# Memory attention and a squared-ReLU MLP: padded state rows with whole-tile weight halves, and the squared ReLU kept in PSUM

## The chip, the cores and the metric

The kernel runs on one core of a Trainium2 chip. Its metric is device time in microseconds (us) of one execution. The engines of a core work side by side, each through its own queue in order: TensorE (PE, with its weight loads as PEld), VectorE (DVE), ScalarE (ACT), GpSimd (POOL) and SyncE (SP), which here only issues DMAs.

## The reference

```python
scale = 1.0 / np.sqrt(D)                     # x: (8, 8, 512, 64), state: (8, 8, 32, 64): B, H, S or N, D
a  = softmax(scale * x @ state.T)            # rows of x read the state
a2 = softmax(scale * state @ x.T)            # rows of the state read x
attn = concat([a @ state, a2 @ x], axis=2)   # (8, 8, 544, 64)
h = attn.transpose(0, 2, 1, 3).reshape(8 * 544, 512) @ w_in    # w_in (512, 2048)
g = np.maximum(h, 0.0) ** 2
out = g @ w_out                              # w_out (2048, 512)
```

Both softmaxes subtract the row's maximum and add 1e-9 to the sum. x, state and the output are float32; the weights arrive as float64.

## The kernel before

TensorE multiplies float32r, a shortened float32, at full speed. So a factor that must be exact is divided into hi, the value rounded to float32r, and lo, the rest; a product becomes hi·hi + lo·hi + hi·lo. The helper `split` does it: ACT casts into hi, another engine subtracts to get lo.

The rows of x never pass through `a @ state` followed by w_in. Instead z = state @ w_in is formed for each head, and up(x) = a @ z. `z_part(G, k, g)` makes one part of z: G is the group of four batches (0: batches 0 to 3, 1: batches 4 to 7), k one of 8 blocks of 256 columns of w_in, g one of two halves of the rows. For G = 0 its `convert` turns the float64 words of w_in into float32 (`singles`: one ACT and four VectorE instructions, lines 106 to 116) and keeps the result in DRAM (`wd`); for G = 1 it is loaded from there. `cut` divides the weights: a tile w2 of 128 rows holds, for one head of a pair, hi of that head's 64 rows and lo of the same rows in the other 64. `product(i)` multiplies it with the state: once with stz_lo and once with stz_hi, both of which hold the state twice, in rows 0 to 63 and again in 64 to 127 (`z_state`). So each product of the array adds hi and lo of the weights. The first six parts of G = 0 are `plain`: one float32 product, undivided. z goes to DRAM (`zd`) and comes back, re-ordered, by `z_fetch`.

The MLP works in units. A unit is 128 of the 2048 columns of h for one batch: `up` adds six products of 128x512 into the PSUM tile ph (pool ps_h, two buffers). Then ACT takes the ReLU into r in SBUF, the square follows in place (ACT in the first ten units, then VectorE at line 383), and `split` gives g_hi (ACT) and g_lo. g_lo is computed by VectorE, in the first, third and fifth unit by POOL. r, g_hi and g_lo have two buffers each. `down` adds twelve products of 128x512 into four tiles po, two units later: eight that read g_hi, four that read g_lo. Batches 0 and 1 are done in pieces, `BOTH`, while the weights are still being converted: 2 units of batch 0, 6 of batch 1, 14 of batch 0, 10 of batch 1. The last 16 units are half as wide and do the state's own rows.

`wo_load` converts w_out in the same way as w_in (tile wof). Steps that are not units (conversion, z, attention of the coming batches) are handed out between units by two lists with due times, `weights` and `reads`. This gives the program's order; a scheduler then fixes each engine's queue from it and from its own timing of instructions, so an edit in one place can move instructions in others. The tags and pools set which buffers a step waits for: w2_0 and w2_1 have two buffers, wf two.

Of the kernel before, what the change touches and what calls it, by code (L numbers as in the profile page):

```python
# [18 lines left out]
def memory_attention_then_relu2_ffn(  # L19
# [21 lines left out]
    nc = tc.nc  # L41
# [80 lines left out]
    def z_state(G):  # L122
        if G == 0:
            raw = const.tile([P, H, GB * N], F32, name="st_f")
            st["raw"] = raw
        else:
            raw = sb.tile([P, H, GB * N], F32, name="st_raw", tag="raw", bufs=RAW)
        src = stT.rearrange("d (h b n) -> d h b n", h=H, b=B)[:, :, G * GB:(G + 1) * GB, :]
        for j in range(2):
            nc.sync.dma_start(  # L130
                out=raw[j * D:(j + 1) * D].rearrange("d h (b n) -> d h b n", b=GB), in_=src
            )
        hi = sb.tile([P, H, GB * N], F32R, name="stz_hi", bufs=1)
        lo = sb.tile([P, H, GB * N], F32R, name="stz_lo", bufs=1)
        split(hi, lo, raw, nc.gpsimd)
        st[G] = hi, lo

    def z_part(G, k, g):

        box = {}  # L140
        ccs = slice(g * NCC // NG, (g + 1) * NCC // NG)
        nq = NCC // NG

        def load():
            if G:
                box["wf"] = sb.tile([P, nq, FW], F32, name="wf", bufs=2)
                nc.sync.dma_start(out=box["wf"], in_=wd[k][:, ccs, :])
                return
            raw = sb.tile([P, nq, FW, 2], I32, name="w_raw", tag="raw", bufs=RAW)
            nc.sync.dma_start(out=raw.rearrange("p c f w -> p (c f w)"), in_=w_in[k * NG + g])  # L150
            box["raw"] = raw

        def convert():
            wf = sb.tile([P, nq, FW], F32, name="wf", bufs=2)
            singles(wf, box["raw"])
            nc.sync.dma_start(out=wd[k][:, ccs, :], in_=wf)
            box["wf"] = wf

        plain = G == 0 and k * NG + g < PLAIN_Z

        def cut():
            if plain:
                return
            wf = box["wf"]
            w2 = []
            for i in range(2):
                own = slice(i * D, (i + 1) * D)
                other = slice((1 - i) * D, (2 - i) * D)
                w = sb.tile([P, nq, FW], F32R, name=f"w2_{i}", bufs=2)
                nc.scalar.copy(out=w[own], in_=wf[own])  # L170
                nc.gpsimd.tensor_sub(out=w[other], in0=wf[own], in1=w[own].bitcast(F32))  # L171
                w2.append(w)
            box["w2"] = w2

        def product(i):
            def run():
                own = slice(i * D, (i + 1) * D)
                pz = ps_x.tile([P, nq, FW], F32, name="pz", tag="px")
                for q in range(nq):
                    h = g * HG + 2 * q + i  # L180
                    if plain:
                        nc.tensor.matmul(
                            pz[:, q, :], lhsT=st["raw"][own, h, :], rhs=box["wf"][own, q, :],
                            start=True, stop=True,
                        )
                        continue
                    st_hi, st_lo = st[G]
                    w = box["w2"][i][:, q, :]
                    nc.tensor.matmul(pz[:, q, :], lhsT=st_lo[:, h, :], rhs=w, start=True, stop=False)  # L189
                    nc.tensor.matmul(pz[:, q, :], lhsT=st_hi[:, h, :], rhs=w, start=False, stop=True)  # L190
                if G == 0 and k == 0:
                    if g == 0 and i == 0:
                        z_first.append(sb.tile([P, NG, FW], F32, name="z_raw", bufs=2))
                    for q in range(nq):
                        at = (2 * q + i) * N
                        dst = z_first[0][at:at + N, g, :]
                        nc.scalar.copy(out=dst, in_=pz[:N, q, :])
                stage = sb.tile([P, nq, FW], F32, name="z_stage", bufs=4)
                nc.scalar.copy(out=stage, in_=pz)
                dst = zd[G, k].rearrange("p g (q i) f -> p g q i f", i=2)[:, g, :, i, :]  # L200
                nc.scalar.dma_start(out=dst, in_=stage)
            return run

        return load, convert, cut, [product(i) for i in range(2)]
# [161 lines left out]
    def mlp(width, fcs, first, rows, aux, at_end=None):  # L366

        nt = width // P
        po = []
        gs = {}  # L370
        last = len(fcs) - 1

        def up(fc):
            ph = ps_h.tile([P, S], F32, name="ph", tag="ph")[:, :width]
            todo = first(fc)
            for i, (w, v) in enumerate(todo):
                nc.tensor.matmul(ph, lhsT=w, rhs=v, start=i == 0, stop=i == len(todo) - 1)  # L377
            r = sb.tile([P, S], F32, name="r", bufs=2)[:, :width]
            nc.scalar.activation(r, ph, AF.Relu)  # L379
            if units[0] < 10:  # L380
                nc.scalar.activation(r, r, AF.Square)
            else:
                nc.vector.tensor_mul(out=r, in0=r, in1=r)  # L383
            units[0] += 1
            hi = sb.tile([P, S], F32R, name="g_hi", bufs=2)[:, :width]
            lo = sb.tile([P, S], F32R, name="g_lo", bufs=2)[:, :width]
            split(hi, lo, r, pool_early(units[0] < 6 and units[0] % 2))
            gs[fc] = hi, lo

        def down(i):  # L390
            fc = fcs[i]
            hi, lo = gs.pop(fc)
            if not po:
                po.extend(
                    ps_o.tile([P, DM], F32, name=f"po{t}", tag="po") for t in range(nt)
                )
            todo = [(t, j) for t in range(nt) for j in range(3)]
            if i < last:
                todo.sort(key=lambda tj: tj[1] == 2)
            for t, j in todo:  # L400
                g = (hi, hi, lo)[j][:, t * P:(t + 1) * P]
                w = wo[fc // FPC][j % 2][:, fc % FPC, :]
                nc.tensor.matmul(  # L403
                    po[t], lhsT=g, rhs=w, start=i == 0 and j == 0, stop=i == last and j == 2
                )

        for i in range(len(fcs) + 2):
            if i <= last:
                up(fcs[i])
                aux()  # L410
            elif i == last + 1 and at_end:
                at_end()
            if i >= 2:
                down(i - 2)
            if i <= last:
                aux()
        for t in range(nt):
            rows(t, po[t])
# [253 lines left out]
```

## Time and profile before

| What | Value |
|---|---|
| median of 3 runs | 738.25 us (737.76 to 740.44) |
| the profiled execution | 736.62 us; span from the first instruction to the last 734.8 us |
| mean granted TensorE clock | 0.97 |
| PE busy | 678.6 us (92%), 3112 instructions |
| DVE busy | 520.5 us (71%), 774 instructions |
| ACT busy | 403.1 us (55%), 720 instructions |
| POOL busy | 259.0 us (35%), 201 instructions |
| DMA moved | 94.71 MB, mean 129 GB/s |

Busy time is the union of an engine's instructions. In rows of instructions, "L97 DVE ... g_lo<-r,g_hi 128x512 ... x16 | 20.3, 1272 | 3.5" reads: line 97 on VectorE, output g_lo from inputs r and g_hi, 16 of them, 20.3 us in all, 1272 ns the mean of one, and 3.5 us in which the engine idled just before them. Line 97 is that of the helper `split`, so its rows are told apart by their tiles. Instructions of one engine that follow each other closely overlap a little at their ends, so their starts lie closer than their durations.

### The profile page before, as it was taken

To read this page: it belongs to the slowest core of one execution; us is meant where nothing else is said; L and a number is where in the kernel's file an instruction comes from. 1 tells how busy PE (TensorE), PEld (TensorE's weight loads), DVE (VectorE), ACT (ScalarE), POOL (GpSimd) and SP (SyncE) were. 2 spreads that over 40 slices of the span, in tenths; PEclk is the share of its full clock that TensorE was granted. 3 is DMA by queue.
4 is the path that set the end of the run, shared out by engine and by line. 5 is a ranking of instruction groups with operands and counts; after the bars stand their busy time and mean duration, and the time that the engine had idled before them with its cause. 6 is when DMAs were issued, how large, how long until landed. Compare 5 with 4: busy or idle time off the path is not lost.

```text
span 734.8 us, 9269 instructions
## 1 busy us (share of the span) xinstructions
PE 678.6 (92%) x3112; PEld 548.6 (75%) x3112; DVE 520.5 (71%) x774; ACT 403.1 (55%) x720; POOL 259.0 (35%) x201
## 2 busy tenths in 40 slices
PE   4877878868999999999999999999999999999994
PEld 2456666656788788888888888888888888888993
DVE  5998999895978789648854984498459745442542
ACT  3748696554666767677643653465345434332541
POOL 3456556664655763752250332033212400000000
PEclk9769999998999999999999999999999999999998
DMA  9878788555553653464232212221121102100420
GB/s 295 267 250 293 214 258 273 186 159 163 175 167 128 214 184 111 139 219 132 87 88 82 89 58 70 77 84 68 62 85 51 38 29 86 35 10 0 144 58 29
DMA packets 74163, 94.71 MB, mean 129 GB/s; under 512 B 3972, under 2 KB 55940, under 8 KB 74116
## 3 DMA queue, kind: packets, MB, share of 16 engines
q1 hardware_dynamic: 56708, 77.34, 33.1%
q10 hardware_dynamic: 17408, 16.78, 6.7%
q8 instruction: 24, 0.39, 0.2%
q14 instruction: 23, 0.19, 0.1%
HBM read 62.13 MB, written 31.98 MB: 128 GB/s over the span
## 4 chain that ended last, share of the span: by engine, by line
PE 67%; DVE 6%; DMA 3%; ACT 2%; issue 1%; POOL 0%; ACTq 0%; DVEq 0%; POOLq 0%; SPq 0%
PE po L403 41%; PE ph L377 21%; DMA z_raw<-zd 3%; PE pr L340 2%; PE pq L274 1%; DVE r L383 1%; DVE g_lo L97 1%; DVE wof L112 1%; PE pz L190 1%; PE pz L189 1%; DVE z_lo L97 1%; PE pt L328 1%; DVE wof L108 1%; DMA zd<-z_stage 0%; DVE wof L107 0%
## 5 line engine op out<-in xcount | busy, mean ns | idle before, releaser
L403 PE MATMUL po<-wo_hi,g_hi 128*128 128x512 f32 x544 | 215.1, 397 | 3.2 <-ACT wo_hi L96 2.2
L403 PE MATMUL po<-wo_lo,g_hi 128*128 128x512 f32 x544 | 214.7, 396 | 0.0
L383 DVE TENSOR_TENSOR r<-r 128x512 f32<-128x512 f32 (+1 forms) x134 | 112.4, 840 | 98.5 <-ACT r L379 98.4
L97 DVE TENSOR_TENSOR g_lo<-r,g_hi 128x512 fp32r<-128x512 f32 (+1 forms) x141 | 120.0, 852 | 64.4 <-PE po L403 44.9
L403 PE MATMUL po<-wo_hi,g_lo 128*128 128x512 f32 x544 | 156.6, 397 | 6.4 <-DVE g_lo L97 6.3
L379 ACT ACTIVATE r<-ph 128x512 f32<-128x512 f32 (+1 forms) x144 | 82.0, 572 | 119.0 <-PE ph L377 108.1
L96 ACT CAST g_hi<-r 128x512 fp32r<-128x512 f32 (+1 forms) x144 | 85.9, 597 | 90.3 <-DVE r L383 51.5
L403 PEld LDWEIGHTS po<-wo_hi,g_lo 128*128 128x128 f32 x544 | 101.0, 189 | 29.9 <-DVE g_lo L97 9.2
L403 PEld LDWEIGHTS po<-wo_hi,g_hi 128*128 128x128 f32 x544 | 102.9, 189 | 25.8 <-ACT wo_hi L96 2.8
L403 PEld LDWEIGHTS po<-wo_lo,g_hi 128*128 128x128 f32 x544 | 102.8, 189 | 21.7 <-issue 0.7
L171 POOL TENSOR_TENSOR w<-wf,w 64x512 fp32r<-64x512 f32 x52 | 79.1, 1521 | 45.0 <-ACT w L170 26.6
L377 PE MATMUL ph<-a_hi,z_hi 128*128 128x512 f32 x256 | 84.5, 408 | 8.1 <-ACT r L379 4.0
L377 PE MATMUL ph<-a_lo,z_hi 128*128 128x512 f32 x256 | 82.8, 399 | 0.0
L377 PE MATMUL ph<-a_hi,z_lo 128*128 128x512 f32 x256 | 82.1, 401 | 0.0
L97 POOL TENSOR_TENSOR xt_hl<-xt_raw,xt_hl 128x1024 fp32r<-128x1024 f32 x12 | 29.9, 2494 | 114.9 <-ACT xt_hl L96 87.4
L377 PEld LDWEIGHTS ph<-a_hi,z_hi 128*128 128x128 f32 x256 | 47.8, 193 | 19.8 <-ACT r L379 5.5
L97 POOL TENSOR_TENSOR xn_hl<-xn_raw,xn_hl 128x1024 fp32r<-128x1024 f32 x16 | 40.4, 2525 | 49.7 <-ACT xn_hl L96 49.0
L377 PEld LDWEIGHTS ph<-a_hi,z_lo 128*128 128x128 f32 x256 | 49.3, 194 | 10.7
L377 PEld LDWEIGHTS ph<-a_lo,z_hi 128*128 128x128 f32 x256 | 48.7, 192 | 10.8
L97 DVE TENSOR_TENSOR z_lo<-z_raw,z_hi 128x512 fp32r<-128x512 f32 x64 | 50.2, 785 | 7.6 <-ACT z_hi L96 7.6
L96 ACT CAST z_hi<-z_raw 128x512 fp32r<-128x512 f32 x64 | 39.4, 615 | 12.7 <-DMA z_raw<-zd 12.7
L97 POOL TENSOR_TENSOR a_lo<-at,a_hi 128x512 fp32r<-128x512 f32 x16 | 24.0, 1498 | 55.1 <-ACT a_hi L96 55.0
(125 smaller groups left out, 865.9 us busy)
## 6 DMA issues: line engine op xcount, KB each, us to landing
zd<-z_stage ACTq DMA_DIRECT2D x64, 256.0 KB
z_raw<-zd SPq DMA_DIRECT2D x63, 256.0 KB
xt_raw<-xT SPq DMA_DIRECT2D x16, 512.0 KB
w_raw<-w_in SPq DMA_DIRECT2D x16, 512.0 KB
wo_raw<-w_out SPq DMA_DIRECT2D x16, 512.0 KB
xn_raw<-xn SPq DMA_DIRECT2D x16, 512.0 KB
wd<-wf SPq DMA_DIRECT2D x16, 256.0 KB
wf<-wd SPq DMA_DIRECT2D x16, 256.0 KB
```

The costliest lines, as they stand in the source:

```text
L96: nc.scalar.copy(out=hi, in_=src)
L97: eng_lo.tensor_sub(out=lo, in0=src, in1=hi.bitcast(F32))
L108: nc.vector.tensor_scalar(out=bits, in0=bits, scalar1=3, scalar2=0x3FFFFFF8, op0=ALU.logical_shift_left, op1=ALU.bitwise_and,)
L112: nc.vector.scalar_tensor_tensor(out=bits, in0=high, scalar=-0x40000000, in1=bits, op0=ALU.bitwise_and, op1=ALU.bitwise_or,)
L171: nc.gpsimd.tensor_sub(out=w[other], in0=wf[own], in1=w[own].bitcast(F32))
L189: nc.tensor.matmul(pz[:, q, :], lhsT=st_lo[:, h, :], rhs=w, start=True, stop=False)
L190: nc.tensor.matmul(pz[:, q, :], lhsT=st_hi[:, h, :], rhs=w, start=False, stop=True)
L340: nc.tensor.matmul(pr[:, q].rearrange("p i c -> p (i c)"), lhsT=my["e"][:, t, q].rearrange("p i n -> p (i n)"), rhs=my["xn"][:, t, q].rear ...
L377: nc.tensor.matmul(ph, lhsT=w, rhs=v, start=i == 0, stop=i == len(todo) - 1)
L379: nc.scalar.activation(r, ph, AF.Relu)
L383: nc.vector.tensor_mul(out=r, in0=r, in1=r)
L403: nc.tensor.matmul(po[t], lhsT=g, rhs=w, start=i == 0 and j == 0, stop=i == last and j == 2)
```

## The change

For batches 0 to 3 (G = 0) the weights are divided once: w2_0 holds hi of all 128 rows, w2_1 holds lo, and `split` makes them with one ACT cast and one VectorE subtraction of 128x512. Before, ACT made two casts and POOL two subtractions of 64x512. The state is padded: stz_hi and stz_lo of a head hold the state in that head's own 64 rows and zeros in the other 64 (four memsets on POOL, and two casts and two subtractions on half the rows). Since a product no longer adds hi and lo of the weights by itself, there are three products a head: lo·hi, hi·hi, hi·lo. Batches 4 to 7 keep their way, and so do the six plain parts.

In the MLP the square is written back into the PSUM tile ph: ACT's Square reads r and writes ph in the first ten units, VectorE multiplies ph by r into ph in the others (a negative value times its ReLU is zero). `split` reads ph in place of r, always with VectorE.

```diff
--- before.py
+++ after.py
@@ -132,7 +132,15 @@
             )
         hi = sb.tile([P, H, GB * N], F32R, name="stz_hi", bufs=1)
         lo = sb.tile([P, H, GB * N], F32R, name="stz_lo", bufs=1)
-        split(hi, lo, raw, nc.gpsimd)
+        if G:
+            split(hi, lo, raw, nc.gpsimd)
+        else:
+            for i in range(2):
+                own = slice(i * D, (i + 1) * D)
+                other = slice((1 - i) * D, (2 - i) * D)
+                for v in (hi, lo):
+                    nc.gpsimd.memset(v[other, i::2, :].bitcast(F32), 0.0)
+                split(hi[own, i::2, :], lo[own, i::2, :], raw[own, i::2, :], nc.vector)
         st[G] = hi, lo
 
     def z_part(G, k, g):
@@ -162,15 +170,16 @@
             if plain:
                 return
             wf = box["wf"]
-            w2 = []
-            for i in range(2):
+            w2 = [sb.tile([P, nq, FW], F32R, name=f"w2_{i}", bufs=2) for i in range(2)]
+            box["w2"] = w2
+            if G == 0:
+                split(w2[0], w2[1], wf, nc.vector)
+                return
+            for i, w in enumerate(w2):
                 own = slice(i * D, (i + 1) * D)
                 other = slice((1 - i) * D, (2 - i) * D)
-                w = sb.tile([P, nq, FW], F32R, name=f"w2_{i}", bufs=2)
                 nc.scalar.copy(out=w[own], in_=wf[own])
                 nc.gpsimd.tensor_sub(out=w[other], in0=wf[own], in1=w[own].bitcast(F32))
-                w2.append(w)
-            box["w2"] = w2
 
         def product(i):
             def run():
@@ -185,9 +194,16 @@
                         )
                         continue
                     st_hi, st_lo = st[G]
-                    w = box["w2"][i][:, q, :]
-                    nc.tensor.matmul(pz[:, q, :], lhsT=st_lo[:, h, :], rhs=w, start=True, stop=False)
-                    nc.tensor.matmul(pz[:, q, :], lhsT=st_hi[:, h, :], rhs=w, start=False, stop=True)
+                    u, v = (w[:, q, :] for w in box["w2"])
+                    todo = ((st_lo, u), (st_hi, u), (st_hi, v))
+                    if G:
+                        w = box["w2"][i][:, q, :]
+                        todo = (st_lo, w), (st_hi, w)
+                    for j, (a, w) in enumerate(todo):
+                        nc.tensor.matmul(
+                            pz[:, q, :], lhsT=a[:, h, :], rhs=w,
+                            start=j == 0, stop=j == len(todo) - 1,
+                        )
                 if G == 0 and k == 0:
                     if g == 0 and i == 0:
                         z_first.append(sb.tile([P, NG, FW], F32, name="z_raw", bufs=2))
@@ -378,13 +394,13 @@
             r = sb.tile([P, S], F32, name="r", bufs=2)[:, :width]
             nc.scalar.activation(r, ph, AF.Relu)
             if units[0] < 10:
-                nc.scalar.activation(r, r, AF.Square)
+                nc.scalar.activation(ph, r, AF.Square)
             else:
-                nc.vector.tensor_mul(out=r, in0=r, in1=r)
+                nc.vector.tensor_mul(out=ph, in0=ph, in1=r)
             units[0] += 1
             hi = sb.tile([P, S], F32R, name="g_hi", bufs=2)[:, :width]
             lo = sb.tile([P, S], F32R, name="g_lo", bufs=2)[:, :width]
-            split(hi, lo, r, pool_early(units[0] < 6 and units[0] % 2))
+            split(hi, lo, ph, nc.vector)
             gs[fc] = hi, lo
 
         def down(i):
```

VectorE in the weight stage, around the g_lo of one of the first six units: wof is a tile of w_out, wf one of w_in, z_lo the rest of a fetched z. Before:

```order
L97 TENSOR_TENSOR g_lo<-r,g_hi 128x512
L116 SCALAR_TENSOR_TENSOR wf<-w_raw,wf 128x512
L107 TENSOR_SCALAR wof<-wof 128x512
L108 TENSOR_SCALAR wof<-wof 128x512
L97 TENSOR_TENSOR z_lo<-z_raw,z_hi 128x512
L112 SCALAR_TENSOR_TENSOR wof<-wo_raw,wof 128x512
```

And now:

```order
L97 TENSOR_TENSOR g_lo<-ph,g_hi 128x512
L108 TENSOR_SCALAR wf<-wf 128x512
L107 TENSOR_SCALAR wof<-wof 128x512
L112 SCALAR_TENSOR_TENSOR wf<-w_raw,wf 128x512
L108 TENSOR_SCALAR wof<-wof 128x512
L97 TENSOR_TENSOR w_1_749<-wf,w_0_748 128x512
L116 SCALAR_TENSOR_TENSOR wf<-w_raw,wf 128x512
```

The cut of the weights (w_1 from wf and w_0) now stands among the conversions, and g_lo reads ph.

POOL in the same stage, where wo_lo is the rest of a tile of w_out. Before:

```order
L171 TENSOR_TENSOR w_0_511<-wf,w_0_511 64x512
L171 TENSOR_TENSOR w_1_514<-wf,w_1_514 64x512
L97 TENSOR_TENSOR wo_lo_311<-wof,wo_hi_310 128x512
L97 TENSOR_TENSOR g_lo<-r,g_hi 128x512
L171 TENSOR_TENSOR w_0_562<-wf,w_0_562 64x512
L171 TENSOR_TENSOR w_1_565<-wf,w_1_565 64x512
```

And now:

```order
L97 TENSOR_TENSOR a_lo<-at,a_hi 128x512
L97 TENSOR_TENSOR wo_lo_317<-wof,wo_hi_316 128x512 x2
L97 TENSOR_TENSOR wo_lo_502<-wof,wo_hi_501 128x512 x2
L97 TENSOR_TENSOR wo_lo_624<-wof,wo_hi_623 128x512 x2
L97 TENSOR_TENSOR wo_lo_796<-wof,wo_hi_795 128x512 x2
```

Between the conversions of w_out, POOL's queue has nothing left of the cuts of G = 0 or of g_lo.

TensorE late in the kernel, in a stretch of units with nothing between them: ph are the up products of a unit, po the down products of the unit two before. Before:

```order
L377 MATMUL ph<-a_hi,z_hi 128x512 x2
L377 MATMUL ph<-a_hi,z_lo 128x512 x2
L377 MATMUL ph<-a_lo,z_hi 128x512 x2
L403 MATMUL po_5716<-wo_hi_310,g_hi 128x512
L403 MATMUL po_5716<-wo_lo_311,g_hi 128x512
L403 MATMUL po_5717<-wo_hi_310,g_hi 128x512
```

And now:

```order
L419 MATMUL po_5744<-wo_lo_317,g_hi 128x512
L419 MATMUL po_5745<-wo_hi_316,g_hi 128x512
L393 MATMUL ph<-a_hi,z_hi 128x512 x2
L393 MATMUL ph<-a_hi,z_lo 128x512 x2
L393 MATMUL ph<-a_lo,z_hi 128x512 x2
L419 MATMUL po_5745<-wo_lo_317,g_hi 128x512
L419 MATMUL po_5742<-wo_hi_316,g_lo 128x512
```

The up products stood ahead of all the down products of the unit two before. They now stand behind seven of its eight that read g_hi, and ahead of the four that read g_lo.

## The prediction

> **What bounds the kernel now.** I read the engine rows and the slices of the page first, then busy time by stretch, then the groups of instructions inside the stretch that is not full on TensorE, then the order of time in two places there.
>
> ```profile
> PE   4877878868999999999999999999999999999994
> DVE  5998999895978789648854984498459745442542
> DMA  9878788555553653464232212221121102100420
> ```
> ```profile
> 0.00:20.00 20.00, 10.72 (x22) 5.49 (x23) 12.12 (x29) 8.81 (x17) 7.20 (x11) 0.89 0.92 302
> 20.00:60.00 40.00, 30.30 (x90) 18.13 (x89) 39.90 (x65) 24.86 (x48) 21.76 (x15) 0.76 0.81 264
> 60.00:100.00 40.00, 32.78 (x144) 26.43 (x143) 36.72 (x44) 30.37 (x56) 23.44 (x16) 0.91 0.80 251
> 100.00:140.00 40.00, 33.69 (x154) 26.15 (x152) 38.76 (x54) 25.55 (x46) 23.91 (x12) 1.00 0.71 233
> 140.00:170.00 30.00, 21.82 (x98) 17.40 (x99) 26.98 (x29) 18.69 (x33) 19.72 (x16) 0.94 0.62 187
> 170.00:200.00 30.00, 25.27 (x117) 19.89 (x116) 20.56 (x24) 15.63 (x27) 15.80 (x13) 0.94 0.49 150
> ...
> 200.00:690.00 490.00, 489.44 (x2283) 404.37 (x2282) 328.56 (x499) 264.10 (x462) 147.19 (x120) 1.00 0.29 94
> ```
>
> The columns of the second fence are busy time of PE, PEld, DVE, ACT and POOL, then the granted clock, the DMA share and GB/s. There are two regimes. From 200 to 690 us TensorE is busy 489.44 of 490 us: nothing that the other engines save there is worth anything, and only a new wait of TensorE could show. From 20 to 170 us, the stage in which the weights are converted, TensorE is busy 118.6 of 150 us and VectorE 39.90 + 36.72 + 38.76 + 26.98 = 142.4 us, 95%. This stage belongs to VectorE's queue. What the change takes out of that queue brings everything behind it forward, and the full stretch begins earlier.
>
> What VectorE does there, out of the groups by shape from 20 to 170 us, with POOL's groups of the same stretch behind them:
>
> ```profile
> L97 DVE TENSOR_TENSOR g_lo<-r,g_hi 128x512 fp32r<-128x512 f32 x16 | 20.3, 1272 | 3.5 <-ACT g_hi L96 3.5
> L112 DVE SCALAR_TENSOR_TENSOR wof<-wo_raw,wof 128x512 int32<-128x512 int32 x16 | 18.9, 1182 | 0.2
> L116 DVE SCALAR_TENSOR_TENSOR wf<-w_raw,wf 128x512 int32<-128x512 int32 x14 | 15.1, 1081 | 0.1
> L97 DVE TENSOR_TENSOR z_lo<-z_raw,z_hi 128x512 fp32r<-128x512 f32 x10 | 11.8, 1179 | 0.4 <-ACT z_hi L96 0.4
> L112 DVE SCALAR_TENSOR_TENSOR wf<-w_raw,wf 128x512 int32<-128x512 int32 x14 | 11.0, 784 | 0.1
> L108 DVE TENSOR_SCALAR wof<-wof 128x512 int32<-128x512 int32 x16 | 10.7, 668 | 0.2
> L108 DVE TENSOR_SCALAR wf<-wf 128x512 int32<-128x512 int32 x14 | 10.1, 720 | 0.1
> L107 DVE TENSOR_SCALAR wf<-wf 128x512 f32<-128x512 f32 x14 | 9.6, 685 | 0.2 <-ACT wf L106 0.2
> L383 DVE TENSOR_TENSOR r<-r 128x512 f32<-128x512 f32 x9 | 8.5, 942 | 0.0
> L107 DVE TENSOR_SCALAR wof<-wof 128x512 f32<-128x512 f32 x16 | 7.6, 474 | 1.9 <-ACT wof L106 1.9
> L97 DVE TENSOR_TENSOR e_hl<-pt,e_hl 128x512 fp32r<-128x512 f32 x2 | 1.4, 686 | 0.8 <-ACT e_hl L96 0.8
> ```
> ```profile
> L171 POOL TENSOR_TENSOR w<-wf,w 64x512 fp32r<-64x512 f32 x23 | 37.3, 1623 | 22.3 <-issue 7.8 <-ACT w L170 6.4 <-PE ph L377 5.7
> ...
> L97 POOL TENSOR_TENSOR g_lo<-r,g_hi 128x512 fp32r<-128x512 f32 x3 | 4.2, 1401 | 4.6 <-ACT g_hi L96 2.8 <-issue 1.8
> ```
>
> The same subtraction costs 1.272 us when both inputs lie in SBUF (g_lo, z_lo 1.179) and 0.686 us when one lies in PSUM (e_hl, out of pt). After POOL has fallen idle, z_lo is as short (600 to 690 us):
>
> ```profile
> L97 DVE TENSOR_TENSOR z_lo<-z_raw,z_hi 128x512 fp32r<-128x512 f32 x7 | 4.8, 686 | 0.3 <-ACT z_hi L96 0.3
> ```
>
> So the excess is POOL's doing, and an operand in PSUM escapes it. One stretch in order of time shows both at once, VectorE first, then POOL:
>
> ```profile
> 197.26 1.28 DVE L596 TENSOR_TENSOR so_far<-so_far,po 128x512 f32<-128x512 f32 x2
> 198.45 2.33 DVE L97 TENSOR_TENSOR g_lo<-r,g_hi 128x512 fp32r<-128x512 f32 x1
> ...
> 197.81 2.42 POOL L97 TENSOR_TENSOR xt_hl<-xt_raw,xt_hl 128x1024 fp32r<-128x1024 f32 x1 [4.12 <-issue]
> ```
>
> Two additions with po (PSUM) run at 0.64 us each across the start of POOL's xt_hl; the g_lo behind them, all in SBUF, does not end until 200.78, 0.55 us after POOL's 200.23.
>
> **The change part by part**, in VectorE's queue up to about 170 us.
>
> The subtraction g_lo reads ph instead of r: 16 × (1.272 − 0.686) = 9.4 us less. The multiplication (nine of them) reads one input in PSUM and writes PSUM. No row writes PSUM from VectorE, so its ends are 0.686 (e_hl) and 0.942 (itself now); I take 0.686, since the input side is what POOL delays: 9 × 0.256 = 2.3 us less. The three early g_lo of POOL come to VectorE: 3 × 0.686 = 2.1 us more. The lower half of the weights, 10 tiles of 128x512, comes to VectorE as one subtraction with both inputs in SBUF: between 0.686 and 1.179 each (the two z_lo rows); I take 0.9, between them because POOL stays but is less busy: 9.0 us more. The padded state's two subtractions: 2 × 0.69 = 1.4 us more. The four memsets fall to POOL at the very start, where it is busy 7.20 of 20 us, and nothing reads them before the seventh part of w_in; they cost nothing.
>
> POOL loses 20 of the 23 groups at L171 (three belong to batches 4 to 7) and three g_lo: 20 × 1.623 + 4.2 = 36.7 of its 21.76 + 23.44 + 23.91 + 19.72 = 88.8 us, 41%. The conversions and z_lo now carry an excess over clean durations (0.686 for three-operand groups, 0.474 as an upper bound for L107 and L108): 16 × 0.496 + 14 × 0.395 + 10 × 0.493 + 14 × 0.098 + 16 × 0.194 + 14 × 0.246 + 14 × 0.211 = 29 us. If that excess shrinks with POOL's load, 41% of it, 12 us, goes; if POOL's remaining work merely falls on other instructions, nothing does. I take 10, nearer the upper end, because these cuts stand among the conversions.
>
> Sum for VectorE: −9.4 − 2.3 + 2.1 + 9.0 + 1.4 − 10 = −9.2 us. The ends are −13.2 (cuts at 0.686, relief 12) and +5.9 (cuts at 1.179, no relief, multiplication at 0.942).
>
> By the Trainium skill (Perfetto Trace Analysis, "Optimizing Scalar/DVE Operations") a VectorE access pays about 125 ns of overhead on PSUM against about 60 on SBUF, which speaks against this change. The trace does not show it: 686 ns with PSUM, 686 without. By that page the 28 moved instructions of the stage (16 + 3 + 9) would give back 28 × 0.065 = 1.8 us, an estimate from its figures, and VectorE's sum would be −7.4: still inside the forecast's own range.
>
> TensorE gets three products for two: 10 parts × 4 tiles = 40 more of 128x256, at this distance of starts in the chain that ended last (its third row is twelve down products of 512 columns, used below):
>
> ```profile
> 197.01 0.12 PE pz L189
> 197.13 0.12 PE pz L190
> ...
> 655.01 2.75 PE po L403 x12
> ```
>
> 40 × 0.12 = 4.8 us, in a stage in which TensorE idles 31 us; only the last part's four, 0.5 us, stand on the path, since the next unit waits for that part's trip through DRAM, which the change leaves alone. ACT casts each part once instead of twice and is busy 99.5 of 150 us: no term. No DMA is added or taken away; SP and ACT issue the same transfers. Net: −9.2 + 0.5 = −8.7 us.
>
> The wait that is added: ph has two buffers and was free after relu; now g_lo is its last reader, so the up products of unit k wait for g_lo of unit k−2, and all that is queued behind them on TensorE waits too (down products, z products, and through the two w2 buffers the next cut, now on VectorE). In the full stretch the order has moved: the up products, now behind seven of unit k−2's products with g_hi, begin 7 × 0.23 = 1.6 us later. The tightest place now, and the usual one:
>
> ```profile
> 405.78 0.62 PE L377 MATMUL ph<-a_hi,z_hi 128*128 128x512 f32 x2
> ...
> 406.51 1.88 DVE L97 TENSOR_TENSOR g_lo<-r,g_hi 128x512 fp32r<-128x512 f32 x1
> ...
> 655.11 0.60 ACT L379 ACTIVATE r<-ph 128x512 f32<-128x512 f32 x1 [1.73 <-PE ph L377]
> ...
> 657.87 0.69 DVE L97 TENSOR_TENSOR g_lo<-r,g_hi 128x512 fp32r<-128x512 f32 x1 [0.83 <-PE po L403]
> ```
>
> At 405.78 the up products start 2.61 us before the g_lo of two units earlier ends (408.39). With g_lo at 0.69 it ends 1.2 us earlier, and the order gives 1.6: covered by 0.2 us. Late in the kernel the chain from relu to g_lo takes 657.87 + 0.69 − 655.11 = 3.45 us, against 6.9 us from the end of a unit's up products to the start of those two units on (30 products at 2.75/12 = 0.23, the last row of the chain above). I cost the wait at nothing; if the cover is gone, each such place costs up to 2.6 us.
>
> **The rivals.** (1) The lock only moves: the cuts on VectorE meet POOL's wo_lo and a_lo at 1.179, and the relief is half, 5 us: −9.4 − 2.3 + 2.1 + 11.8 + 1.4 − 5 + 0.5 = −0.9 us, 737, no change. For it: z_lo has just this form and is at 1.179. Against: POOL loses 41% of its work.
> (2) It becomes slower through the held ph tile. In the weight stage g_lo trails far behind, and each pair of units must now fit the up products (6 × 0.23 = 1.4 us) between one g_lo and the relu two units on, where so far they ran ahead; some 22 units, 11 pairs, give 15 us, and VectorE idles behind a cut that waits for a late product. 738.25 − 8.7 + 15 = 745. It decides from 9 us on. For it: ACT already waits for g_lo through r's two buffers, the same loop,
>
> ```profile
> ACT r L379 <- DVE g_lo L97: 9.9, 10, 2.2
> ```
>
> ten times in the whole kernel, 9.9 us together. Against: just that smallness, and that conversions independent of the units can fill VectorE's queue. The Trainium skill (PSUM — Partial Sum Buffer, "Summary: rules for kernel authors") says to evacuate PSUM promptly, which this change does not.
> (3) More comes: the excess is concentrated on POOL's cuts, and relief is 20 of the 29 us, cuts at 0.75: 738.25 − 8.7 − 10 − 1.5 = 718.
>
> **How the numbers follow.** The profiled execution took 736.62 us with a span of 734.8; the median shown is 738.25, 1.6 above it. The sum is a difference inside the span: 734.8 − 8.7 = 726.1, and 738.25 − 8.7 = 729.5 on the scale of the median. Under 0.5% (3.7 us) I call no change, about what a measurement of this kernel can tell. Chances: the forecast (724 to 734) 0.54; (1) 0.20; (2) 0.14; (3) 0.12. Faster by over 0.5%: 0.54 + 0.12 = 0.66; within: 0.20; slower: 0.14. The range leaves out (2) and the far half of (3): 720 to 740. The case that I forecast has 724 to 734 of its own.
>
> **What would show it.** After the change, from 20 to 170 us: g_lo and the multiplication near 0.69; the cut on VectorE between 0.69 and 1.18; L112 on wof and L116 on wf clearly under 1.18 and 1.08; TensorE's full stretch beginning some 9 us before 200. Wrong steps would show as: the cut at 1.18 and conversions as long as now (rival 1); idle time of PE before ph put down to g_lo, in the weight stage or once a batch (rival 2), g_lo at 0.75 or more (PSUM costs VectorE more after all). What would make the prediction wrong is above all a VectorE queue that idles behind a cut whose w2 buffer is not free.

## The result and the profile after

The change makes the kernel slower: 745.52 us median of 11 runs (740.68 to 749.12) against 738.88 us (736.06 to 742.68) of the kernel before in the same comparison, a ratio of 1.0077 (95% interval 1.0048 to 1.0106). The prediction said 729.5 us. The profiled execution of the changed kernel took 741.56 us with a span of 739.7, 4.9 above the 734.8 of the kernel before. It lies near the low end of its runs, so what it shows is rather less than what a median run loses.

The slices of the page after, then busy time by stretch, in the same stretches and columns as in the prediction:

```profile
PE   4866979886999999999998999999999999999994
...
DVE  5999897843668588438859687468454345443552
```

```profile
0.00:20.00 20.00, 8.97 (x16) 3.90 (x16) 12.25 (x26) 7.76 (x15) 6.42 (x14) 0.90 0.93 296
20.00:60.00 40.00, 31.27 (x86) 18.72 (x86) 38.51 (x68) 22.59 (x44) 17.37 (x12) 0.71 0.73 228
60.00:100.00 40.00, 30.89 (x135) 25.23 (x136) 37.04 (x62) 29.55 (x55) 8.60 (x7) 0.91 0.88 286
100.00:140.00 40.00, 35.12 (x177) 29.09 (x176) 32.99 (x56) 24.75 (x48) 6.84 (x6) 0.99 0.80 258
140.00:170.00 30.00, 27.82 (x140) 23.27 (x139) 18.03 (x27) 18.71 (x32) 13.44 (x13) 0.96 0.62 169
170.00:200.00 30.00, 23.33 (x106) 18.98 (x105) 13.14 (x20) 11.59 (x22) 11.95 (x13) 0.89 0.46 142
200.00:690.00 490.00, 485.19 (x2253) 401.65 (x2251) 299.82 (x493) 259.78 (x459) 133.24 (x120) 1.00 0.29 93
```

VectorE's work did what was predicted, and more. From 20 to 170 us it is busy 38.51 + 37.04 + 32.99 + 18.03 = 126.6 us instead of 142.4. TensorE got nothing from it by the time the full stretch begins: the relu of unit 21 starts at 180.2 us instead of 184.0, but that of unit 28 at 219.3 instead of 219.7, so what had been won is lost again in between (units are counted from 0). From 20 to 170 us TensorE is busy 125.1 us instead of 118.6, of which the added products take 4.8; it does less than before from 0 to 20 us (8.97 for 10.72) and from 170 to 200 us (23.33 for 25.27); and in the stretch that was full, 200 to 690 us, it now lacks 4.8 us (0.6 before). VectorE's groups from 20 to 170 us:

```profile
L112 DVE SCALAR_TENSOR_TENSOR wof<-wo_raw,wof 128x512 int32<-128x512 int32 x16 | 13.5, 843 | 0.2
L97 DVE TENSOR_TENSOR g_lo<-ph,g_hi 128x512 fp32r<-128x512 f32 x19 | 13.0, 685 | 2.0 <-ACT g_hi L96 1.7
...
L399 DVE TENSOR_TENSOR ph<-ph,r 128x512 f32<-128x512 f32 x10 | 6.9, 694 | 4.1 <-ACT r L395 4.1
L97 DVE TENSOR_TENSOR z_lo<-z_raw,z_hi 128x512 fp32r<-128x512 f32 x10 | 6.9, 688 | 10.9 <-ACT z_hi L96 10.7
L97 DVE TENSOR_TENSOR w<-wf,w 128x512 fp32r<-128x512 f32 x10 | 6.8, 685 | 0.6 <-ACT w L96 0.5
```

g_lo is at 685 ns, the cut (w) at 685, the multiplication at 694, z_lo at 688 instead of 1179, L112 on wof at 843 instead of 1182. Of the eight groups of conversions six became shorter and two longer (L112 on wf 1001 for 784, L116 on wof 866 for 743). Where the saved time went is told by the waits of the same stretch (who waited for whom: us in total, times, longest):

```profile
ACT z_hi L96 <- DMA z_raw<-zd: 23.0, 7, 4.9
...
DVE z_lo L97 <- ACT z_hi L96: 10.7, 4, 4.4
PE po L419 <- ACT g_hi L96: 9.1, 5, 4.0
...
PE ph L393 <- DVE g_lo L97: 2.2, 1, 2.2
```

z_lo waited 0.4 us before and now waits 10.7: VectorE stands idle behind z_lo, z_lo behind z_hi on ACT, and z_hi behind the trip of z through DRAM. TensorE's wait for g_hi before its down products was not in this stretch before at all and is 9.1 us now. The wait that the prediction had looked for, ph for g_lo, is 2.2 us, once. From 170 to 690 us the same wait of TensorE for g_hi stands twice more:

```profile
PE po L419 <- ACT g_hi L96: 9.6, 2, 5.0
```

The first of the two, in order of time (ph are the up products of units 20 and 21, the last two of this part of batch 0; po their down products):

```profile
179.14 0.62 ACT L96 CAST z_hi<-z_raw 128x512 fp32r<-128x512 f32 x1 [2.24 <-DMA z_raw<-zd]
...
179.66 1.08 ACT L395 ACTIVATE r<-ph 128x512 f32<-128x512 f32 x2
...
180.40 1.29 DVE L399 TENSOR_TENSOR ph<-ph,r 128x512 f32<-128x512 f32 x2
...
184.71 0.62 ACT L96 CAST z_hi<-z_raw 128x512 fp32r<-128x512 f32 x1 [3.97 <-DMA z_raw<-zd]
185.24 0.58 ACT L96 CAST g_hi<-ph 128x512 fp32r<-128x512 f32 x1
...
185.87 0.79 PE L419 MATMUL po<-wo_hi,g_hi 128*128 128x512 f32 x1 [4.98 <-ACT g_hi L96]
185.97 0.69 DVE L97 TENSOR_TENSOR g_lo<-ph,g_hi 128x512 fp32r<-128x512 f32 x1
...
189.45 1.43 PE L419 MATMUL po<-wo_hi,g_lo 128*128 128x512 f32 x4
...
190.71 0.62 PE L393 MATMUL ph<-a_hi,z_hi 128*128 128x512 f32 x2
```

ACT does the two relu at 179.66, VectorE squares both by 181.69. Then the next instruction in ACT's queue is not g_hi of unit 20 but a z_hi whose tile is still on its way through DRAM; it starts at 184.71. g_hi follows at 185.24, and TensorE has waited 4.98 us. It had nothing else to do: the up products of unit 22 need the ph of unit 20, which is held until its g_lo (185.97), and so they come at 190.71, behind the down products of unit 20.

The second place is the boundary from batch 3 to batch 4. Beside POOL's xn_hl and what follows it there, two small VectorE operations on sp_hl take 3.71 us. Behind them in VectorE's queue stand the steps up to nm of the coming batch's attention; on ACT, e (which waits for nm) stands ahead of the relu of units 64 and 65:

```profile
396.39 2.45 POOL L97 TENSOR_TENSOR xn_hl<-xn_raw,xn_hl 128x1024 fp32r<-128x1024 f32 x1 [6.24 <-ACT xn_hl L96]
...
396.56 3.71 DVE L251 SCALAR_TENSOR_TENSOR sp_hl<-sp_raw,sp_hl 64x128 fp32r<-64x128 f32 x2
...
402.95 0.63 PE L393 MATMUL ph<-a_lo,z_hi 128*128 128x512 f32 x2
402.99 0.65 DVE L307 TENSOR_REDUCE nm<-st 128x1 f32<-128x512 f32 x1
...
403.67 0.72 ACT L310 ACTIVATE e<-st,nm 128x512 f32<-128x512 f32 x1 [2.07 <-DVE nm L307]
...
404.99 1.09 ACT L395 ACTIVATE r<-ph 128x512 f32<-128x512 f32 x2
...
406.00 0.69 DVE L399 TENSOR_TENSOR ph<-ph,r 128x512 f32<-128x512 f32 x1
...
407.94 1.11 ACT L96 CAST g_hi<-ph 128x512 fp32r<-128x512 f32 x2
...
408.62 0.29 PEld L419 LDWEIGHTS po<-wo_hi,g_hi 128*128 128x128 f32 x1 [4.84 <-ACT g_hi L96]
```

The up products were done at 403.58, their squares are made from 406.00, g_hi from 407.94, and TensorE waits 4.60 us. What each wait costs beyond itself is seen in the windows of the two waits and of the stretches behind them (the number behind POOL's busy time is the granted clock):

```profile
181.00:185.80 4.80, 0.00 (x0) 0.00 (x0) 1.72 (x4) 1.09 (x3) 0.00 (x0) 0.75 0.58 162
185.80:190.70 4.90, 4.83 (x12) 3.84 (x13) 2.15 (x4) 2.34 (x5) 3.55 (x5) 0.55 0.27 95
404.00:408.60 4.60, 0.02 (x1) 0.00 (x0) 4.60 (x11) 4.58 (x11) 0.00 (x0) 1.00 0.45 171
408.60:413.40 4.80, 4.78 (x19) 4.06 (x20) 3.81 (x9) 0.52 (x2) 0.00 (x0) 0.64 0.31 96
```

In the stretches behind the waits the mean granted clock is 0.55 and 0.64, which makes 4.9 × 0.45 = 2.2 and 4.8 × 0.36 = 1.7 us more. Together the two places take 5.0 + 2.2 + 4.6 + 1.7 = 13.5 us, and the span is 4.9 us longer than before, so in this execution the rest of the kernel is 8.6 us faster.

### The profile page after: what moved, and what is told of

Same layout as the page of the kernel before. It is cut to its first block, busy times and chain, and to the rows that moved or that the text cites. A ratio compares the mean times of both kernels' runs of the same rounds, so it can differ in the third digit from the quotient of the medians.

```text
span 739.7 us, 9320 instructions
## 1 busy us (share of the span) xinstructions
PE 682.1 (92%) x3152; PEld 556.0 (75%) x3152; DVE 472.0 (64%) x789; ACT 392.0 (53%) x711; POOL 197.9 (27%) x181
## 5 line engine op out<-in xcount | busy, mean ns | idle before, releaser
L419 PE MATMUL po<-wo_hi,g_hi 128*128 128x512 f32 x544 | 221.6, 408 | 20.7 <-ACT g_hi L96 18.7
L419 PE MATMUL po<-wo_lo,g_hi 128*128 128x512 f32 x544 | 219.3, 403 | 0.0
L399 DVE TENSOR_TENSOR ph<-ph,r 128x512 f32<-128x512 f32 (+1 forms) x134 | 88.8, 664 | 156.7 <-ACT r L395 156.4
L419 PEld LDWEIGHTS po<-wo_hi,g_hi 128*128 128x128 f32 x544 | 105.3, 194 | 45.7 <-ACT g_hi L96 21.6
L419 PEld LDWEIGHTS po<-wo_lo,g_hi 128*128 128x128 f32 x544 | 105.8, 194 | 21.9 <-POOL wo_lo L97 0.4
L97 DVE TENSOR_TENSOR g_lo<-ph,g_hi 128x512 fp32r<-128x512 f32 (+1 forms) x144 | 94.5, 657 | 37.1 <-ACT g_hi L96 32.0
L96 ACT CAST g_hi<-ph 128x512 fp32r<-128x512 f32 (+1 forms) x144 | 81.1, 564 | 47.5 <-DVE ph L399 40.6
L393 PE MATMUL ph<-a_hi,z_hi 128*128 128x512 f32 x256 | 82.0, 401 | 7.3 <-ACT a_hi L96 3.4
L97 DVE TENSOR_TENSOR z_lo<-z_raw,z_hi 128x512 fp32r<-128x512 f32 x64 | 52.3, 818 | 21.1 <-ACT z_hi L96 20.9
L182 POOL TENSOR_TENSOR w<-wf,w 64x512 fp32r<-64x512 f32 x32 | 42.9, 1342 | 28.2 <-ACT w L181 24.1
L215 ACT COPY z_stage<-pz 128x512 f32<-128x512 f32 x64 | 37.6, 588 | 11.1 <-PE pz L203 9.9
```

Source lines behind the costliest of these rows:

```text
L96: nc.scalar.copy(out=hi, in_=src)
L97: eng_lo.tensor_sub(out=lo, in0=src, in1=hi.bitcast(F32))
L399: nc.vector.tensor_mul(out=ph, in0=ph, in1=r)
L419: nc.tensor.matmul(po[t], lhsT=g, rhs=w, start=i == 0 and j == 0, stop=i == last and j == 2)
```

## The experiments

Medians and ratios are against runs of the kernel before on the same chip (738.7 to 739.7 us).

**The halves alone.** Edits against the kernel before. The first, with the z half untouched:

```diff
-                nc.scalar.activation(r, r, AF.Square)
+                nc.scalar.activation(ph, r, AF.Square)
-                nc.vector.tensor_mul(out=r, in0=r, in1=r)
+                nc.vector.tensor_mul(out=ph, in0=ph, in1=r)
-            split(hi, lo, r, pool_early(units[0] < 6 and units[0] % 2))
+            split(hi, lo, ph, nc.vector)
```

> Only the MLP half of the change: squared ReLU kept in PSUM and all g_lo on VectorE; padding, division and products of z as before. Theory H (held ph): because g_lo is now the last reader of ph, the up products of a unit are placed behind products of the unit two earlier, TensorE loses about a unit of lead over relu, multiplication and g_hi, and each delay of that chain now shows; this half alone should cost what the whole change costs, 742 to 748 us against some 738.9 before, with waits of PE for g_hi around 400 to 420 us. Rival Z (the z half costs it: three products, subtractions of w and state in VectorE's queue): this half alone keeps only the shorter g_lo and gives 731 to 737 us.

Measured: 732.73 us, ratio 0.9917 (0.9899 to 0.9934).

The second has all the rest of the change (z_state, cut, product) and not these lines.

> Only the z half of the change: padded state, w divided once in place on VectorE, three products a head; squared ReLU in SBUF and g_lo as before. Theory H (held ph): 733 to 740 us, since ph is free after relu as before and POOL has less to do. Rival Z: the loss lies here, 743 to 748 us, with the first full slice of TensorE later than before.

Measured: 735.62 us, ratio 0.9956 (0.9937 to 0.9974). Each half alone makes the kernel faster, and neither theory had both. Only the two together make it slower.

**The whole change with ph free.**

```diff
-                nc.scalar.activation(ph, r, AF.Square)
+                nc.scalar.activation(r, r, AF.Square)
-                nc.vector.tensor_mul(out=ph, in0=ph, in1=r)
+                nc.vector.tensor_mul(out=r, in0=ph, in1=r)
-            split(hi, lo, ph, nc.vector)
+            split(hi, lo, r, pool_early(units[0] < 6 and units[0] % 2))
```

> The whole change, except that the square is written to r in SBUF (Square from r to r, multiplication of ph by r into r), g_hi and g_lo read r, and the early g_lo of POOL stay there: ph is free after the multiplication, and g_lo has both inputs in SBUF again. Theory H (held ph): 733 to 740 us, no wait of PE for g_hi near 400 us, although g_lo is long again (1.0 to 1.3 us beside POOL). Rival Z: 743 to 748 us, as after, or more, since g_lo takes longer.

Measured: 730.95 us, ratio 0.9884 (0.9859 to 0.9909), below the range given.

**Where the hold costs.** In the next three the condition c picks the units whose square goes to r; in the others it goes to ph (the early Square on ACT and the source of `split` follow the same condition and are left out here).

```diff
-                nc.vector.tensor_mul(out=ph, in0=ph, in1=r)
+                nc.vector.tensor_mul(out=r if c else ph, in0=ph, in1=r)
```

> The whole change, but for units 60 to 67 (the four on each side of the boundary from batch 3 to batch 4) the square goes to r in SBUF, so that ph is free after the multiplication there; 120 of the 128 units of the batches hold ph to g_lo as in the change. Theory S (one meeting place: at the boundary at 404 us the attention of batch 5, drawn forward by the held ph, stands ahead of the relu of units 64 and 65 on ACT, and TensorE idles 4.6 us and then runs at a lower clock): 731 to 736 us. Rival T (the loss lies in the first 200 us, where both halves of the change meet): 741 to 747 us, as after.

Measured: 747.37 us, ratio 1.0113 (1.0088 to 1.0138). Theory S in this form is wrong. The wait at 404 us is gone, but the one of unit 20 is still there and a new one of 4.1 us, which ends at 484 us, has come at the next boundary of batches (from 170 to 690 us, both together):

```profile
PE po L420 <- ACT g_hi L96: 9.3, 2, 5.2
```

> The whole change with ph held to g_lo in the first 32 units (batches 0 and 1, the weight stage); from unit 32 on the square goes to r in SBUF and ph is free after the multiplication. Theory S (the boundary at 404 us): 728 to 734 us, as the kernel with ph free everywhere (730.95) or a little less, since g_lo is short where POOL is busy. Rival T (the first 200 us): 740 to 746 us.

Measured: 740.62 us, ratio 1.0032 (1.0015 to 1.0050).

> The reverse: ph free after the multiplication in the first 32 units, held to g_lo in all later ones; TensorE's order around units 64 to 66 is then the one of the whole change. Theory S: 738 to 746 us, with PE waiting 4 us or more for g_hi near 404 us. Rival T: 728 to 734 us.

Measured: 735.69 us, ratio 0.9972 (0.9953 to 0.9990). The wait at the boundary to batch 4 is as in the whole change:

```profile
PE po L420 <- ACT g_hi L96: 6.5, 2, 4.6
```

With ph free the time is 730.95; ph held in the first 32 units adds 9.7, held in the later ones 4.7; together that makes 745.4, and the whole change takes 745.5. So both stretches count, the first for about twice the second, and rival T was nearer than theory S: the first kernel lies in T's range, the second between the two ranges. The next kernel leaves the hold and shifts the attention:

```diff
-        reads.add(order(b), 2 * begins[b] - 1, 2 * ends[b - 2])
+        reads.add(order(b), 2 * begins[b] - 1, 2 * ends[b - 2] + 2)
```

> The whole change, ph held everywhere; only the steps of the attention of batches 2 to 7 may begin one unit later than now, so that the attention of batch 5 stands elsewhere around the boundary at 404 us. Theory S: the wait of TensorE for g_hi there goes or falls under 2 us, 731 to 737 us. Rival T: 741 to 747 us.

Measured: 745.03 us (741.34 to 745.58, 4 runs), ratio 1.0074 (1.0053 to 1.0094). The wait near 404 us did shrink, to 0.7 us, and that of unit 20 is 6.2 us. That the total did not fall is not explained: TensorE's order is that of the whole change up to 256 us, and yet the wait of unit 20 ends at 193.4 us here, at 190.7 in the kernel with units 60 to 67 free, at 190.9 in the one held in the first 32 units, whose orders are also the same there, and at 185.9 in the whole change's profiled execution. So the first part of one and the same order scatters by several us from one execution to another, and the one profiled of the whole change was an early one.

**Is it the hold, or the PSUM operand?** Here ph is held and the squares are in SBUF:

```diff
-            split(hi, lo, ph, nc.vector)
+            nc.scalar.copy(out=hi, in_=r)
+            nc.vector.scalar_tensor_tensor(
+                out=lo, in0=r, scalar=ph[:, :1], in1=hi.bitcast(F32),
+                op0=ALU.bypass, op1=ALU.subtract,
+            )
```

> The z half of the change as it is; the square goes to r in SBUF and g_hi is cast from r, but g_lo (r - g_hi, all in SBUF, same values) also names one column of ph that it does not use, so that ph is held to g_lo without any large operand in PSUM there. Theory H (the hold, through the order of TensorE that it forces): 740 to 748 us, against 731.0 with ph free after the multiplication. Rival P (the hold is harmless; squares written to PSUM and read from it are what slows the chain): 729 to 734 us.

Measured: 733.76 us, ratio 0.9928 (0.9906 to 0.9950). Theory H, that the hold costs wherever it is, is wrong: ph is held in all units, and there is no long wait, since in this order nine down products of unit 19 stand between the up products of unit 21 and the down products of unit 20: from 170 to 690 us TensorE waits 1.7 us for g_hi, in two pieces. The time lies in rival P's range, but P's reason does not follow: from 20 to 170 us the multiplication into PSUM (694 ns) is as long as the one into SBUF here (681), g_lo out of PSUM is shorter (685 ns for 1120), and a kernel with the squares in PSUM comes to 734.46 below.

**The old z half with ph free.** One operand, against the kernel before:

```diff
-                nc.vector.tensor_mul(out=r, in0=r, in1=r)
+                nc.vector.tensor_mul(out=r, in0=ph, in1=r)
```

> The kernel before with one edit: the multiplication reads ph (PSUM) and r instead of r twice; the result stays in r, the z half is as before. If the hold costs the same whatever the z half is (9.7 us in the first 32 units, 4.7 later, as found by freeing each), the MLP half with the hold, 732.7, should fall to about 718 us here. If the hold costs only together with the new z half, this kernel is at 730 to 736 us.

Measured: 732.97 us, ratio 0.9914 (0.9894 to 0.9935). So with the old z half the hold, together with the shorter g_lo that comes with it, costs nothing that can be seen (732.73 with both), and this one operand brings nearly as much as any other kernel here.

**Which part of the z half?**

```diff
-                split(w2[0], w2[1], wf, nc.vector)
+                split(w2[0], w2[1], wf, nc.gpsimd)
```

> The whole change with one edit: the lower half of the divided weights (w2_1) is subtracted on POOL instead of VectorE; padding, three products and held ph stay. Theory C (the cuts in VectorE's queue delay relu's square and g_lo, which the held ph turns into waits): 730 to 738 us. Rival O (the forced order and the third product alone): 742 to 748 us.

Measured: 736.10 us, ratio 0.9955 (0.9940 to 0.9971). This is in theory C's range, but not clearly for its reason: TensorE still waits 11.1 us for g_hi from 20 to 170 us (9.1 in the whole change), and what went are the two long waits behind 170 us (9.6 to 1.9 us, longest 0.8). The cut was moved, and with it the order everywhere.

> The whole change, but the square goes to r in SBUF (multiplication of ph by r), g_hi and g_lo read r, and all g_lo are on VectorE, the early ones too: ph is free after the multiplication, and this differs from the change in nothing but where the square lies. Theory H (the hold): 729 to 735 us. If the place of the three early g_lo was what helped the kernel with ph free, 738 us or more.

The edit is that of the kernel with ph free, with `split(hi, lo, r, nc.vector)`. Measured: 730.44 us, ratio 0.9878 (0.9853 to 0.9903): with the first kernel with ph free (730.95) the fastest of the study. The place of the early g_lo was not what helped. It has the same z_hi in the same place of ACT's queue as the whole change:

```profile
181.36 1.28 DVE L399 TENSOR_TENSOR r<-ph,r 128x512 f32<-128x512 f32 x2
...
182.10 0.30 PEld L393 LDWEIGHTS ph<-a_hi,z_hi 128*128 128x128 f32 x2 [0.84 <-DVE r L399]
...
184.51 0.62 PE L393 MATMUL ph<-a_lo,z_hi 128*128 128x512 f32 x2
185.66 0.62 ACT L96 CAST z_hi<-z_raw 128x512 fp32r<-128x512 f32 x1 [3.96 <-DMA z_raw<-zd]
186.18 0.61 ACT L96 CAST g_hi<-r 128x512 fp32r<-128x512 f32 x1
...
186.85 0.51 PE L419 MATMUL po<-wo_hi,g_hi 128*128 128x512 f32 x1 [1.71 <-ACT g_hi L96]
```

z_hi waits for its transfer as in the whole change and g_hi of unit 20 comes at 186.18, as late after the squares. But ph was free after the multiplication, the up products of units 22 and 23 run from 182.10 to 185.13, and of the 5 us TensorE loses 1.71.

**One place.** With the hold everywhere, only this z_hi and its z_lo leave ACT and VectorE:

```diff
+        if (b, k) == (1, 4):
+            nc.gpsimd.tensor_copy(out=hi, in_=raw)
+            nc.gpsimd.tensor_sub(out=lo, in0=raw, in1=hi.bitcast(F32))
+        else:
             split(hi, lo, raw, nc.vector)
```

> The whole change with ph held everywhere; one division of z (batch 1, the ninth and tenth unit: z_hi and z_lo, one tile each) goes to POOL instead of ACT and VectorE, so that it no longer stands, waiting for its transfer, ahead of g_hi of unit 20. The order around the boundary at 404 us also comes out otherwise (the products of unit 66 after two of unit 64, not after eight and the reads). Theory A (single meeting places: a queue's head waits for a transfer or for VectorE where the held ph leaves TensorE nothing else): the waits of 5 us at 181 and 404 us go, 732 to 738 us. Theory H (the hold costs everywhere): 742 to 747 us.

Measured: 734.46 us, ratio 0.9927 (0.9902 to 0.9953). One tile of z in 64 moved, and 11 us are gone. TensorE's order is that of the whole change up to unit 23. POOL now waits for the transfer, ACT does g_hi right behind the square, and TensorE waits 1.23 us:

```profile
183.40 1.08 ACT L399 ACTIVATE r<-ph 128x512 f32<-128x512 f32 x2
...
184.14 1.29 DVE L403 TENSOR_TENSOR ph<-ph,r 128x512 f32<-128x512 f32 x2
...
184.86 0.58 ACT L96 CAST g_hi<-ph 128x512 fp32r<-128x512 f32 x1 [0.39 <-DVE ph L403]
...
185.50 0.50 PE L423 MATMUL po<-wo_hi,g_hi 128*128 128x512 f32 x1 [1.23 <-ACT g_hi L96]
...
189.09 0.61 POOL L233 CAST z_hi<-z_raw 128x512 fp32r<-128x512 f32 x1 [8.39 <-DMA z_raw<-zd]
```

The boundary to batch 4 came out in another order too, with the up products of unit 66 behind two down products of unit 64 and not behind all eight. From 170 to 690 us, all waits of TensorE for g_hi:

```profile
PE po L423 <- ACT g_hi L96: 2.4, 3, 1.2
```

Two waits of 5.0 and 4.6 us have become three of 2.4 together, and the clock is 1.00 behind them. By the account above 13.5 − 2.4 = 11.1 us were to be had, and the medians differ by 745.5 − 734.5 = 11.0; that they agree so closely is luck, since the two profiled executions differ by only 7.6 us of span (739.7 and 732.1). Nor are the 11 us all that tile's. From the relu of unit 21 to that of unit 24 the whole change takes 20.4 us, the three kernels with the same order there take 20.4 to 21.5, and this one takes 14.2: at its own place the tile is worth 6 to 7 us. From the relu of unit 60 to the last one it is 346.8 us in the whole change and 340.8 here, and that comes with the other order at the boundary, which the edit did not aim at.

The same edit in the kernel with ph free and all g_lo on VectorE:

> The kernel with ph free and all g_lo on VectorE (730.4), with the same one division of z on POOL. Theory A: TensorE has two further units to run there and loses 1.7 us at that place, so at most 2 us are won: 728 to 732 us. Theory H says the same; if that division costs as much with ph free (5 us or more), both are wrong.

Measured: 732.79 us, ratio 0.9907 (0.9887 to 0.9927), just above the range given, and not clearly apart from 730.44 (the intervals overlap): with ph free, moving that z_hi won nothing. The four kernels together show that it takes both: with ph held and this z_hi on ACT the time is 745.5 us, with only the z_hi moved 734.5, with only ph free 730.4, with both 732.8.

Set side by side, for the kernels with the new z half: TensorE's waits for g_hi before its down products, in the one profiled execution of each.

| kernel | 20 to 690 us | of these, 170 to 690 us | longest | median, us |
|---|---|---|---|---|
| ph free, all g_lo on VectorE | 3.0 | 1.7 | 1.7 | 730.44 |
| ph free, early g_lo on POOL | 1.0 | 0.4 | 0.6 | 730.95 |
| ph free, one z on POOL | 1.9 | 0.4 | 1.0 | 732.79 |
| ph held, squares in SBUF | 2.3 | 1.7 | 1.0 | 733.76 |
| held, one z on POOL | 12.7 | 2.4 | 4.7 | 734.46 |
| z half alone (squares and multiplication all in SBUF) | 1.8 | 0.4 | 0.8 | 735.62 |
| held in later units only | 7.9 | 6.5 | 4.6 | 735.69 |
| held, cut on POOL | 13.0 | 1.9 | 3.2 | 736.10 |
| held in the first 32 units only | 18.5 | 5.7 | 5.7 | 740.62 |
| held, attention a unit later | 18.6 | 6.9 | 6.2 | 745.03 |
| whole change | 18.7 | 9.6 | 5.0 | 745.52 |
| held but at units 60 to 67 | 21.1 | 9.3 | 5.2 | 747.37 |

The sum alone does not order the kernels: 12.7 and 13.0 us go with 734.46 and 736.10, and the MLP half alone, with the old z half, has 11.1 us and takes 732.73. The waits behind 170 us do somewhat better: every kernel above 737 us has 5.7 us or more of them, and of the others only one has more than 2.4.

## Why the prediction was wrong

**The durations** were right. g_lo, with the three from POOL, went from 20.3 to 13.0 us, the 7.3 that the terms −9.4 and +2.1 give. The multiplication is at 694 ns (0.686 taken). PSUM costs VectorE nothing that shows. The Trainium skill (Perfetto Trace Analysis, "Optimizing Scalar/DVE Operations") gives some 65 ns more of overhead for an access to PSUM; g_lo with PSUM at 685 ns and z_lo without at 688 do not bear that out. The cut was mis-sized, in the good direction: 0.685 each, 6.8 us and not 9.0. The relief of the conversions and z_lo was mis-sized too: the nine groups of conversions and z_lo add up to 106.7 us before and 91.1 after, 15.6 us against 10, beyond the upper end of 12. So rival (1) is out, and VectorE is busy 15.8 us less and not 9.2, beyond the far end of −13.2 (whose terms add up to −13.3).

**The step that failed first** is "What the change takes out of that queue brings everything behind it forward, and the full stretch begins earlier". VectorE's 95% was read as the bound. It has 15.8 us less to do from 20 to 170 us, and the relu of unit 28 starts only 0.4 us earlier (in the profiled executions of the three kernels with the same order up to there it starts later, at 223.9 to 227.0). Nor do the other kernels follow VectorE's busy time in that stage: the old z half with one operand of the multiplication changed has 142.5 us of it (before 142.4) and takes 733.0 us; the z half alone has 135.3 and takes 735.6. So the kernels with ph free, which end where the sum said (730.4 for 729.5), are no proof of it. What the saved time became in the changed kernel is waiting: VectorE waits for z_hi, and z_hi for z's trip through DRAM. That is a loop of the conversion, the z product on TensorE, the copy on ACT, two transfers, and the division on ACT and VectorE, which a shorter VectorE can shorten only in part. This is read from the waits; no run shortened the loop.

**The step that turned the sign** is "I cost the wait at nothing". The check behind it was right in itself: ph's own wait for g_lo is 2.2 us, once. It asked whether ph comes free before the up products need it. It did not ask what those up products had been doing there, which is to cover TensorE while relu, square and g_hi of the unit before go through ACT and VectorE. Moved behind the down products they cover nothing. As long as that chain flows, little is lost: in the four kernels that hold ph in all units and have no long wait behind 170 us, TensorE's waits for g_hi there add up to 1.7 to 2.8 us. Where something that waits for a transfer or for the attention stands on ACT ahead of g_hi, or of the relu before it, waits of 4.6 to 5.0 us show, and the clock falls behind them. "ACT ... no term" was part of the same mistake: its busy time did not matter, the head of its queue did.

**Rival (2)** had the time (745) and the resource, the held ph tile. Its wait was another one: it put the loss before ph, in the weight stage, with VectorE idle behind a cut that waits for its buffer. The cut waited 0.6 us in all. So it is luck that its time agrees, though it had the stretch in part: the hold in the first 32 units costs 9.7 us of the 14.4 found. That in the full stretch "only a new wait of TensorE could show" was right, and one did.

What the z half adds to the hold was not separated further. Each half alone and six of the ten edits of the whole change have no such long wait behind 170 us; that the whole change gets two of them was shown, why the scheduler comes to just that order was not. Nor was the remainder settled, some 2 to 4 us between ph held without long waits (733.8, 734.5, 736.1) and ph free (730.4 to 732.8).

## What to carry to other kernels

When a buffer is to be held longer, look not only at whether it comes free in time, but at what the engine that fills it runs while the chain behind the buffer is late; both long waits stood at boundaries of parts, where TensorE had no other work at hand. In a kernel with queues in order, look for a head of queue that waits for a transfer ahead of a short step that another engine waits for. And where a scheduler sets the order, a single edit can move it by more than the edit is worth: here one tile on another engine changed the time by 11 us, some 6 to 7 of them at its own place and the rest through an order that moved elsewhere, so an effect should be tried in two or three neighbouring orders before it is believed.

## What the runs showed of the hardware

Behind the waits of 4.98 and 4.60 us in the whole change the granted clock is 0.50 from 185.8 to 189.4 us and 0.51 from 408.6 to 412.1, and the down products with g_hi stand 0.43 us apart instead of 0.23; from 412.1 on it is 1.00 again. After the wait of 1.23 us the clock stayed at 1.00 and the products 0.23 apart. In the two kernels with ph free, four up products behind a wait of 2.21 us took 1.20 us, and four behind one of 3.36 us took 2.08. The Trainium skill (TensorE: Matmul & The Clock Gate, "Part 1: The HAM clock gate (the "warmup" mystery)") states half the clock after an idle window of about 3.4 us, and the full clock after about 3.4 us of sustained work; the rows agree. By the windows above, each of the two long waits cost some 2 us more than it lasted.

In these runs an operand in PSUM shortened a VectorE operation beside POOL when it was one of the two large ones, and not when it was a column. With a column of ph as the third operand and both tiles in SBUF, g_lo from 20 to 170 us took 1120 ns (mean of 19), not far from the 1272 before:

```profile
L404 DVE SCALAR_TENSOR_TENSOR g_lo<-r,ph,g_hi 128x512 fp32r<-128x512 f32 x19 | 21.3, 1120 | 3.2 <-ACT g_hi L403 3.2
```

With one large operand in PSUM the multiplication took 685 ns over the whole kernel (896 before), in the same kernel in which g_lo, all in SBUF, took 954 (all units of full width):

```profile
L97 DVE TENSOR_TENSOR g_lo<-r,g_hi 128x512 fp32r<-128x512 f32 x125 | 119.1, 954 | 68.7 <-PE po L403 48.3 <-ACT g_hi L96 15.1 <-PE ph L377 2.4
L383 DVE TENSOR_TENSOR r<-ph,r 128x512 f32<-128x512 f32 x118 | 80.8, 685 | 86.3 <-ACT r L379 85.9
```
